# Staged row maxima from 256 keys and 256 key differences instead of 512 keys

## The chip, the cores and the metric

The kernel runs on one core of a Trainium2 chip. The core has a matrix engine (TensorE, PE in the profile, with its weight loads as PEld), a vector engine (VectorE, DVE), a scalar engine (ScalarE, ACT), a general engine (GpSimd, POOL) and a queue that issues transfers (SyncE, SP). ACT can issue transfers as well, from the same in-order queue as its arithmetic. All engines share an on-chip memory (SBUF) of 128 partitions; PE writes its results to PSUM, which DVE and ACT can read. The metric is the device time of one execution in microseconds.

## The reference, cut to what matters

A transformer block: layer norm, attention with 32 heads of 20 columns over 2048 tokens of width 640, a residual, a second layer norm and a SwiGLU feed-forward part.

```
qkv    = layernorm(x) @ wqkv
scores = einsum("bhqd,bhkd->bhqk", q, k) * 20 ** -0.5
p      = softmax(scores, axis=-1)
o      = einsum("bhqk,bhkd->bhqd", p, v)
h      = x + o @ wo
h2     = h + (silu(layernorm(h) @ w_gate) * (layernorm(h) @ w_up)) @ w_down
```

The softmax needs, for every query and head, the maximum over all 2048 keys. All of it is float32; the kernel forms float32 products on PE from a high and a low part of each operand.

## The kernel before, in words

Tokens are cut into four chunks of 512 (`NC`, `CH`) and heads into eight groups of four (`NG`, `G`). One group with one chunk of queries is a *unit* (32 units). The kernel has three stages: the projections (to about 338 us), the attention with the output projection beside it, and the feed-forward part.

**The projections** run over the four chunks. Each chunk has 18 slots: ten *blocks* (`query_key`, L413), each giving 128 output rows of keys (even `m`) or queries (odd `m`) for 512 tokens in 15 matmuls, and eight *value* slots (`value`, 15 matmuls of 320 columns, L469). The first chunk alternates keys and queries; later ones do the five key blocks first and the five query blocks next (the last chunk puts the values between). In the second half of each of the first three chunks, `flip` (L386, transposes at L389) turns the next chunk's normalised tokens.

A block ends in `keep` (L444): ACT and DVE (before slot 8) or ACT and GpSimd (from slot 8) split the result into a high and a low part in one of three buffers `e`, and it is stored to the DRAM tensor `qk_d` of its chunk. `split` is at L79 to L81, `split_sbuf` (a copy out of PSUM first, L265) at L263. The store is issued from ACT's queue (L410), one slot late: `store` issues what the call before has left.

Attention needs the maxima before its exponentials. A part of them is computed inside the projections, 208 *pairs*: one pair is two score matmuls of 128 queries by 512 keys (two heads, 60 rows each, L171, in the two halves of a `ps_wide` tile; three such tiles rotate) and one DVE reduction over both halves (`max_pair`, L175). 60 pairs take keys and queries from the resident tiles `k_stk` and `q_stk` (`unit_keys`); the other 148 take them from *staged* tiles `raw`, 512 keys or 512 queries of one group, read back from `qk_d` (`load_items`, `stack`, issued by SP). Four staged tiles rotate; the next is loaded when all pairs of the fourth before are out. The staged pairs cover groups 1 to 7 for the first chunk's queries and keys, and for the second chunk's queries the keys of the first and a part of the second chunk.

The order is written by hand (`tc.manual_schedule()`): each engine runs its instructions in program order. `visit(n)` puts up to n ready pairs at a place in that order: three after every block or value slot, and, from the second chunk on, one inside each block (after the ninth matmul). In a slot the order is: matmuls, `keep` or the evacuation of the values (L475), `visit(3)`, transfers for the resident tiles, one or two steps of the next chunk's norm on DVE, a flip. So ACT's queue holds a block's copy, split and store issues ahead of anything that the pairs of `visit(3)` bring.

Of the kernel before, what the change touches and what calls it, by code (L numbers as in the profile page):

```python
# [9 lines left out]
F32 = mybir.dt.float32  # L10
# [7 lines left out]
P = 128  # L18
# [11 lines left out]
G = 4  # L30
# [4 lines left out]
ROW = P // 2  # L35
HALF = D // 2
EPS = 1e-5
GD = G * DH

ORDER = ("SmsSMMsWMm", "SsSmWmMs", "SssMWmS")  # L40
# [3 lines left out]
def tile_block(ctx: ExitStack, tc: tile.TileContext, x, wqkv, wo, wg, wu, wd, out):  # L44
# [3 lines left out]
    ctx.enter_context(tc.manual_schedule())  # L48

    dram = ctx.enter_context(tc.tile_pool(name="dram", bufs=1, space=bass.MemoryType.DRAM))  # L50
    qk_d = [dram.tile([2, NG, 2, GD, CH], F32R, name=f"qk_d{c}") for c in range(NC)]
    v_d = dram.tile([S, NG, VG], F32, name="v_d")
    o_d = dram.tile([D, S], F32, name="o_d")
    r_d = dram.tile([H, S], F32, name="r_d")
# [78 lines left out]

    ends = {}

    def stack(dst, which, g, cs):

        src = qk_d[cs.start // CH][which, g].bitcast(F32).rearrange("i (d h) c -> (i d) h c", h=G)
        for b in range(2):
            heads = src[:, 2 * b : 2 * b + 2]  # L140
            both, first = ((DH, 0), (0, 2 * DH))[which]
            for row, n in ((both, 2 * DH), (first, DH)):
                nc.sync.dma_start(
                    dst[b * ROW + row : b * ROW + row + n].bitcast(F32), heads[:n]
                )

    def load_keys(g, cs):

        k = keys[g] = k_stk[g % 2]
        stack(k[:, :, cs], 1, g, cs)  # L150

    def load_queries(u):

        g, c = divmod(u, NC)
        q = queries[u] = stk.tile([P, 2, CH], F32R, name="q_stk", tag="q_stk", bufs=4)
        stack(q, 0, g, slice(c * CH, (c + 1) * CH))

    def load_values(g, t0=0, t1=NT):
        values[g] = v_stk[g % 2]
# [6 lines left out]
    def max_pair(mx, q, k, pair, t, kc, k0):  # L166

        ps = ps_wide()
        for b in range(2):
            rows = slice(b * ROW, b * ROW + NPART)  # L170
            nc.tensor.matmul(  # L171
                ps[:, b, :], q[rows, pair, t * P : (t + 1) * P], k[rows, pair, k0 : k0 + CH],
                start=True, stop=True,
            )
        nc.vector.tensor_reduce(mx[:, :, pair, t, kc], ps, axis=AX.X, op=ALU.max)  # L175

    def max_one(u, kc, t, pair, b):

# [62 lines left out]
    evp_ctx = ExitStack()  # L241
    evp = evp_ctx.enter_context(tc.tile_pool(name="evp", bufs=2))
    evs = [evp.tile([P, NG, VG], F32, name=f"ev{i}", bufs=1) for i in range(2)]
    es = [evp.tile([P, 2, CH], F32R, name=f"e{i}", bufs=1) for i in range(2)]
    es.append(v_stk[0].rearrange("p t w -> p (t w)")[:, : 2 * CH].bitcast(F32R))
    third = es[2] = es[2].rearrange("p (i n) -> p i n", i=2)

    def next_e():
# [3 lines left out]
    with tc.tile_pool(name="pa", bufs=2) as pa:  # L252
# [36 lines left out]
        def load_items():  # L289
            for n, (which, g, c, loaded, _) in enumerate(items):  # L290
                if loaded is not None:
                    continue
                if slot[0] < stored_at(which, g, c) or (n >= 4 and users[n - 4]):
                    return
                t = raw_tile().rearrange("p a b -> p (a b)")[:, : 2 * CH].rearrange(
                    "p (h n) -> p h n", h=2
                )
                stack(t, which, g, slice(c * CH, (c + 1) * CH))
                items[n][3:] = t, slot[0]

        def staged_keys(g, c, kc):
            k, q = place[1, g, (c, kc)], place[0, g, c]

            def one(t, pair):
                max_pair(mxs[g * NC + c], items[q][3], items[k][3], pair, t, kc, 0)
                for n in (k, q):
                    users[n] -= 1
                load_items()

            def ready():  # L310
                return all(items[n][3] is not None and slot[0] >= items[n][4] + 2 for n in (k, q))

            pairs = [(t, pair) for t in moved(g * NC + c, kc) for pair in range(2)]
            for n in (k, q):
                users[n] += len(pairs)
            return [(ready, lambda a=a: one(*a)) for a in pairs]
# [69 lines left out]
        def flip(c, k):  # L386
            ps = ps_one()
            for t in range(TPC):
                nc.tensor.transpose(  # L389
                    ps[:, t * P : (t + 1) * P], xs[c * TPC + t][:, k * P : (k + 1) * P], ident  # L390
                )
            z_hi, z_lo = (z[:, k, :] for z in zs[c])
            split_sbuf(ps, z_hi, z_lo, next_e()[:, 0].bitcast(F32))

        def flip_tokens(t):

# [47 lines left out]
        def keep(c, m, ps):  # L444

            e = next_e()
            if slot[0] < 8:
                split(ps, e[:, 0], e[:, 1], nc.vector)
            else:
                split_sbuf(ps, e[:, 0], e[:, 1], e[:, 1].bitcast(F32))  # L450
            r0 = m // 2 * P
            pieces, r = [], r0
            while r < r0 + P:
                g, i = divmod(r, GD)
                n = min(GD - i, r0 + P - r)
                dst = qk_d[c][1 - m % 2, g].bitcast(F32).rearrange("i r c -> r i c")
                pieces.append((dst[i : i + n], e[r - r0 : r - r0 + n].bitcast(F32)))
                r += n
            store(*pieces, queue=nc.sync if (c, m) == (NC - 1, 2 * ND - 1) else nc.scalar)

        def value(c, t, half):
# [1153 lines left out]
```

## Time and profile before

| | |
|---|---|
| median of the runs shown | 2105.66 us (2105.11 to 2111.35, three runs) |
| the profiled execution's own time | 2112.59 us |
| its span | 2110.5 us |
| granted PE clock, mean | 0.998 |
| projections | from the start to about 338 us |
| DVE reductions of the 208 pairs (L175) | 240.3 us in all |
| ACT in 150 to 200 us | 14.13 of 50 us |

How to read the rows: in a timeline row stand the start, the duration, the engine, the line, what it writes and reads, and how many instructions are merged (x). A bracket gives the idle time before it and what ended that. In a row by groups, the numbers behind the bar are the total busy time and the mean duration in ns, then the idle time before the group and its releasers. The duration of a matmul is modelled and overlaps the next one, so PE's pace is read from start to start.

### The profile page before, as it was taken

How to read it: one execution, taken by the hardware profiler on the slowest of the kernel's cores; microseconds unless marked ns; L12 is line 12 of the kernel's file. 1: busy time of each engine (PE TensorE's matmuls, PEld its weight loads, DVE VectorE, ACT ScalarE, POOL GpSimd, SP SyncE). 2: the span in 40 equal slices, each digit the busy share in tenths (PEclk: the TensorE clock that was granted, in tenths of full speed). 3: DMA queues.
4: the chain of work that ended last, by engine and by line, in shares of the span. 5: the costliest groups of instructions: out<-in, count | busy, mean ns of one | idle time of the engine just before them, and what ended most of it. 6: DMA issues, size and time to landing. Idle time of an engine off the chain costs nothing.

```text
span 2110.5 us, 35624 instructions
## 1 busy us (share of the span) xinstructions
PE 2077.2 (98%) x12636; PEld 1206.5 (57%) x12636; DVE 1753.9 (83%) x2907; ACT 1295.8 (61%) x2571; POOL 694.3 (33%) x1003
## 2 busy tenths in 40 slices
PE   7999999999999999999999999999999999999998
PEld 6666675333333333333333333335578888888888
DVE  7999897999999999999999999996458766666677
ACT  3222216999999998999999999996743222212221
POOL 1122212243343433353420001001135534663555
PEclk9999999999999999999999999999999999999999
DMA  8565532433442524534432113132137755884542
GB/s 260 162 183 167 155 122 82 122 121 107 141 124 97 176 84 133 168 134 131 134 112 70 38 35 90 34 92 84 35 121 258 266 170 187 298 303 158 194 153 94
DMA packets 191633, 295.27 MB, mean 140 GB/s; under 512 B 46840, under 2 KB 81656, under 8 KB 190432
## 3 DMA queue, kind: packets, MB, share of 16 engines
q1 hardware_dynamic: 177872, 266.77, 39.3%
q10 hardware_dynamic: 13584, 26.23, 4.0%
q8 instruction: 101, 1.65, 0.3%
q14 instruction: 76, 0.62, 0.1%
HBM read 196.44 MB, written 95.68 MB: 138 GB/s over the span
## 4 chain that ended last, share of the span: by engine, by line
PE 88%; DVE 6%; DMA 3%; SPq 1%; issue 0%; ACT 0%; POOL 0%; ACTq 0%; POOLq 0%; DVEq 0%
PE acc L917 24%; PE ps_a L1080 15%; PE ps_max L181 15%; PE ps_one L907 15%; PE ps_b L1174 8%; PE ps_one L419 4%; DVE mx L175 4%; PE ps_one L469 2%; PE ps_wide L171 2%; PE ps_max L645 2%; DMA qk_d<-e 1%; PE ps_b L645 1%; DVE mx L187 1%; PE ps_one L389 0%; DMA halves<-j_d 0%
## 5 line engine op out<-in xcount | busy, mean ns | idle before, releaser
L913 ACT ACTIVATE probs<-ps_one 128x512 f32<-128x512 f32 x2048 | 1045.4, 623 | 131.8 <-PE ps_one L907 127.4
L187 DVE TENSOR_REDUCE mx<-ps_max 128x1 f32<-128x512 f32 x1632 | 1020.1, 682 | 96.3 <-PE ps_max L181 54.3
L907 PE MATMUL ps_one<-q_stk,k_stk 62*128 62x512 f32 x2048 | 550.8, 421 | 0.7 <-ACT e L265 0.7
L917 PE MATMUL acc<-probs,v_stk 128*32 128x512 f32 x4096 | 545.2, 605 | 0.3
L181 PE MATMUL ps_max<-k_stk,q_stk 60*128 60x512 f32 x1632 | 540.9, 459 | 2.4 <-DVE mx L187 1.5
L181 PEld LDWEIGHTS ps_max<-k_stk,q_stk 60*128 60x128 f32 x1632 | 230.4, 184 | 428.1 <-DVE mx L187 412.4
L907 PEld LDWEIGHTS ps_one<-q_stk,k_stk 62*128 62x128 f32 x2048 | 299.8, 185 | 81.2 <-ACT probs L913 52.1
L175 DVE TENSOR_REDUCE mx<-ps_wide 128x2 f32<-128x1024 f32 x208 | 240.3, 1216 | 17.6 <-PE ps_wide L171 17.3
L1295 DVE TENSOR_TENSOR tmp<-ps_a,tmp 128x512 f32<-128x512 f32 x208 | 141.2, 689 | 120.1 <-PE ps_a L1080 93.2
L1174 PE MATMUL ps_b<-halves,yp 128*128 128x320 f32 x1032 | 179.3, 308 | 1.9 <-DMA halves<-j_d 1.2
L1174 PEld LDWEIGHTS ps_b<-halves,yp 128*128 128x128 f32 x1032 | 165.1, 188 | 18.5 <-POOL yp L81 1.5
L917 PEld LDWEIGHTS acc<-probs,v_stk 128*32 128x32 f32 x4096 | 80.6, 108 | 160.3 <-issue 152.2
L1080 PE MATMUL ps_a<-t,units 128*128 128x512 f32 x624 | 162.5, 396 | 0.0
L198 POOL CAST both<-neg 128x16 fp32r<-128x16 f32 x32 | 6.6, 206 | 465.0 <-DVE neg L194 222.7
L1080 PE MATMUL ps_a<-z,units 128*128 128x512 f32 x516 | 133.8, 394 | 0.0
L1080 PEld LDWEIGHTS ps_a<-t,units 128*128 128x128 f32 x624 | 112.6, 188 | 18.6
L81 POOL TENSOR_TENSOR yp<-y,yp 128x256 fp32r<-128x256 f32 x96 | 60.2, 627 | 188.1 <-ACT yp L80 188.1
L1179 DVE TENSOR_TENSOR h<-ps_b,h 128x320 f32<-128x320 f32 x248 | 109.9, 480 | 6.8 <-PE ps_b L1174 5.4
L1080 PEld LDWEIGHTS ps_a<-z,units 128*128 128x128 f32 x516 | 93.1, 187 | 15.9
L1080 PE MATMUL ps_a<-z,lasts 128*128 128x512 f32 x324 | 92.5, 393 | 0.0
L80 ACT ACTIVATE yp<-tmp 128x512 fp32r<-128x512 f32 x40 | 25.3, 632 | 103.1 <-POOL tmp L1167 103.1
L265 ACT ACTIVATE e<-ps_one 128x512 f32<-128x512 f32 x31 | 18.5, 598 | 110.0 <-PE ps_one L419 83.0
(169 smaller groups left out, 2059.8 us busy)
## 6 DMA issues: line engine op xcount, KB each, us to landing
units<-w_d SPq DMA_DIRECT2D x186, 256.0 KB
w_d<-stage SPq DMA_DIRECT2D x106, 256.0 KB
halves<-j_d SPq DMA_DIRECT2D x70, 320.0 KB
j_d<-stage SPq DMA_DIRECT2D x42, 320.0 KB
raw<-qk_d SPq DMA_DIRECT2D x70, 160.0 KB
k_stk<-qk_d SPq DMA_DIRECT2D x64, 160.0 KB
q_stk<-qk_d SPq DMA_DIRECT2D x64, 160.0 KB
rb<-r_d SPq DMA_DIRECT2D x32, 256.0 KB
```

The costliest lines, as they stand in the source:

```text
L175: nc.vector.tensor_reduce(mx[:, :, pair, t, kc], ps, axis=AX.X, op=ALU.max)
L181: nc.tensor.matmul(ps, queries[u][rows, pair, t * P : (t + 1) * P], keys[u // NC][rows, pair, kc * CH : (kc + 1) * CH], start=True, stop=True,
L187: nc.vector.tensor_reduce(mxs[u][:, b, pair, t, kc : kc + 1], ps, axis=AX.X, op=ALU.max)
L419: nc.tensor.matmul(ps, w[:, k, m * P : (m + 1) * P], a[:, k, :], start=(n == 0 and k == 0), stop=(n == 2 and k == ND - 1),)
L645: nc.tensor.matmul(ps[:, :HALF], a[:, k, :], w[:, k, hs], start=(n == 0), stop=(n == 3 * ND - 1),)
L907: nc.tensor.matmul(ps, keys[u // NC][rows, p, kt * P : (kt + 1) * P], queries[u][rows, p, :], start=True, stop=True,)
L913: nc.scalar.activation(probs[p][:, b, :], ps, AF.Exp, scale=scale)
L917: nc.tensor.matmul(acc[32 * j : 32 * j + 32, :], values[u // NC][:, kt, j * VW : j * VW + 32], probs[j // 2][:, j % 2, :], start=(kt == 0) ...
L1080: nc.tensor.matmul(ps.rearrange("p (t n) -> p t n", t=TPC), w[k][:, i], z[k][:, :, j], start=(first and m == 0), stop=(last and m == len(n ...
L1174: nc.tensor.matmul(ps, a, b, start=(n == 0), stop=(n == len(pairs) - 1))
L1179: nc.vector.tensor_tensor(out=h, in0=ps, in1=h, op=ALU.add)
L1295: add = lambda out, ps, x: nc.vector.tensor_tensor(out=out, in0=ps, in1=x, op=ALU.add)
```

## The change

Keys of the first two chunks are stored with 256 further columns: for columns i of 0 to 255, key i less key i + 256. `qk_d` becomes two tensors, `q_d` and `k_d`; `k_d` has 768 columns in the first two chunks. A staged key tile now holds columns 256 to 767, that is the second 256 keys and the 256 differences; a score matmul keeps its shape. For a query, the score of a difference is the difference of the two scores, and max(a, b) = b + max(a - b, 0). So in the staged pairs ACT takes the positive part of the 2 x 256 difference scores into an SBUF tile `over` (two rotate), and DVE, once per head, adds it to the 256 scores in PSUM and takes the maximum in the same instruction. The 60 pairs from the resident tiles are as before.

In `keep`, key blocks before slot 8 get a second copy out of PSUM (ACT), a subtraction from PSUM (DVE), and a split by ACT and GpSimd. Key blocks from slot 8 on, in the first two chunks, get a subtraction on GpSimd between the copy and the split, and the split covers 768 columns. Query blocks and the keys of the last two chunks are stored as before. The buffers `e` grow by half, and the parameter `dynamic_dma_scratch_size` is set to 8192, which frees on-chip memory.

```
+LOWEST = -3.4028234e38
...
-    qk_d = [dram.tile([2, NG, 2, GD, CH], F32R, name=f"qk_d{c}") for c in range(NC)]
+    q_d = [dram.tile([NG, 2, GD, CH], F32R, name=f"q_d{c}") for c in range(NC)]
+    k_d = [
+        dram.tile([NG, 2, GD, CH + (CH // 2 if c < 2 else 0)], F32R, name=f"k_d{c}")
+        for c in range(NC)
+    ]
...
-    def stack(dst, which, g, cs):
+    def stack(dst, which, g, c, cols=slice(0, CH)):
 
-        src = qk_d[cs.start // CH][which, g].bitcast(F32).rearrange("i (d h) c -> (i d) h c", h=G)
+        src = (q_d, k_d)[which][c][g].bitcast(F32).rearrange("i (d h) c -> (i d) h c", h=G)
         for b in range(2):
-            heads = src[:, 2 * b : 2 * b + 2]
+            heads = src[:, 2 * b : 2 * b + 2, cols]
...
+    def max_halves(mx, q, k, pair, t, kc):
+
+
+        ps = ps_wide()
+        for b in range(2):
+            rows = slice(b * ROW, b * ROW + NPART)
+            nc.tensor.matmul(
+                ps[:, b, :], q[rows, pair, t * P : (t + 1) * P], k[rows, pair, :],
+                start=True, stop=True,
+            )
+        over = evp.tile([P, 2, CH // 2], F32, name="over")
+        nc.scalar.activation(over, ps[:, :, CH // 2 :], AF.Relu)
+        for b in range(2):
+            nc.vector.tensor_tensor_reduce(
+                over[:, b], ps[:, b, : CH // 2], over[:, b], 1.0, LOWEST, ALU.add, ALU.max,
+                mx[:, b, pair, t, kc : kc + 1],
+            )
...
-    es = [evp.tile([P, 2, CH], F32R, name=f"e{i}", bufs=1) for i in range(2)]
-    es.append(v_stk[0].rearrange("p t w -> p (t w)")[:, : 2 * CH].bitcast(F32R))
+    EW = CH + CH // 2
+    es = [evp.tile([P, 2, EW], F32R, name=f"e{i}", bufs=1) for i in range(2)]
+    es.append(v_stk[0].rearrange("p t w -> p (t w)")[:, : 2 * EW].bitcast(F32R))
...
-                stack(t, which, g, slice(c * CH, (c + 1) * CH))
+                stack(t, which, g, c, slice(CH // 2, EW) if which else slice(0, CH))
...
-                max_pair(mxs[g * NC + c], items[q][3], items[k][3], pair, t, kc, 0)
+                max_halves(mxs[g * NC + c], items[q][3], items[k][3], pair, t, kc)
...
         def keep(c, m, ps):
 
             e = next_e()
+            which, half, n = 1 - m % 2, CH // 2, CH
+            hi, lo = e[:, 0], e[:, 1]
+            copy = lo.bitcast(F32)
+            over = copy[:, CH:]
             if slot[0] < 8:
-                split(ps, e[:, 0], e[:, 1], nc.vector)
+                split(ps, hi[:, :CH], lo[:, :CH], nc.vector)
+                if which:
+                    nc.scalar.activation(over, ps[:, half:], AF.Copy)
+                    nc.vector.tensor_tensor(
+                        out=over, in0=ps[:, :half], in1=over, op=ALU.subtract
+                    )
+                    split(over, hi[:, CH:], lo[:, CH:], nc.gpsimd)
             else:
-                split_sbuf(ps, e[:, 0], e[:, 1], e[:, 1].bitcast(F32))
+                nc.scalar.activation(copy[:, :CH], ps, AF.Copy)
+                if which and c < 2:
+                    nc.gpsimd.tensor_tensor(
+                        out=over, in0=copy[:, :half], in1=copy[:, half:CH], op=ALU.subtract
+                    )
+                    n = EW
+                split(copy[:, :n], hi[:, :n], lo[:, :n], nc.gpsimd)
+            n = EW if which and c < 2 else CH
...
-                dst = qk_d[c][1 - m % 2, g].bitcast(F32).rearrange("i r c -> r i c")
-                pieces.append((dst[i : i + n], e[r - r0 : r - r0 + n].bitcast(F32)))
-                r += n
+                dst = (q_d, k_d)[which][c][g].bitcast(F32).rearrange("i r c -> r i c")
+                pieces.append((dst[i : i + w], e[r - r0 : r - r0 + w, :, :n].bitcast(F32)))
+                r += w
...
-    nc = _bacc.Bacc("TRN2", target_bir_lowering=False, num_devices=1)
+    nc = _bacc.Bacc(
+        "TRN2", target_bir_lowering=False, num_devices=1, dynamic_dma_scratch_size=8192
+    )
```

More of the change, by code (lines that the diff above doesn't have):

```diff
@@ L149, in load_keys @@
         k = keys[g] = k_stk[g % 2]
-        stack(k[:, :, cs], 1, g, cs)
+        stack(k[:, :, cs], 1, g, cs.start // CH)
     def load_queries(u):
@@ L155, in load_queries @@
         q = queries[u] = stk.tile([P, 2, CH], F32R, name="q_stk", tag="q_stk", bufs=4)
-        stack(q, 0, g, slice(c * CH, (c + 1) * CH))
+        stack(q, 0, g, c)
     def load_values(g, t0=0, t1=NT):
@@ L392, in flip @@
             z_hi, z_lo = (z[:, k, :] for z in zs[c])
-            split_sbuf(ps, z_hi, z_lo, next_e()[:, 0].bitcast(F32))
+            split_sbuf(ps, z_hi, z_lo, next_e()[:, 0, :CH].bitcast(F32))
         def flip_tokens(t):
@@ L454, in keep @@
                 g, i = divmod(r, GD)
-                n = min(GD - i, r0 + P - r)
-                dst = qk_d[c][1 - m % 2, g].bitcast(F32).rearrange("i r c -> r i c")
-                pieces.append((dst[i : i + n], e[r - r0 : r - r0 + n].bitcast(F32)))
-                r += n
+                w = min(GD - i, r0 + P - r)
+                dst = (q_d, k_d)[which][c][g].bitcast(F32).rearrange("i r c -> r i c")
+                pieces.append((dst[i : i + w], e[r - r0 : r - r0 + w, :, :n].bitcast(F32)))
+                r += w
             store(*pieces, queue=nc.sync if (c, m) == (NC - 1, 2 * ND - 1) else nc.scalar)
```

## The prediction

> **What bounds the kernel now.** I read the page first, then the stretches of the span, the groups of instructions of the projections, PE's timeline slot by slot, and the chain of waits. From the page:
>
> ```profile
> PE 2077.2 (98%) x12636; PEld 1206.5 (57%) x12636; DVE 1753.9 (83%) x2907; ACT 1295.8 (61%) x2571; POOL 694.3 (33%) x1003
> ```
>
> PE is the limit over the whole, but the change touches only the projections, which end near 338 us. One stretch of them (columns: PE, PEld, DVE, ACT and POOL busy, then clock, DMA share, GB/s):
>
> ```profile
> 150.00:200.00 50.00, 49.00 (x271) 35.67 (x268) 47.61 (x48) 14.13 (x25) 11.61 (x9) 1.00 0.50 163
> ```
>
> DVE is busy for 48 of 50 us, PE for 49, ACT for 14. A faster DVE is worth only what PE waits for it, and that is read from PE's own order. A clean stretch of query or key blocks:
>
> ```profile
> 274.35 0.96 PE L171 MATMUL ps_wide<-raw 60*128 60x512 f32 x6
> ...
> 277.54 0.50 PE L171 MATMUL ps_wide<-raw 60*128 60x512 f32 x2
> ...
> 279.56 0.97 PE L171 MATMUL ps_wide<-raw 60*128 60x512 f32 x6
> ```
>
> The first and the last row are bursts of three pairs of score matmuls after a block, the middle one the single pair inside the next block ("mid"), 3.19 us after the burst began. One block takes 279.56 - 274.35 = 5.21 us and PE never waits in it: an infinitely fast DVE would not shrink it. A clean value slot, with the flip (L389) of one column block in it:
>
> ```profile
> 75.44 0.97 PE L469 MATMUL ps_one<-w_hi,z_hi 128*128 128x320 f32 x5
> ...
> 78.70 0.65 PE L389 MATMUL ps_one<-ident,xt 128*128 128x128 f32 x4
> 79.11 0.97 PE L469 MATMUL ps_one<-w_hi,z_hi 128*128 128x320 f32 x5
> ```
>
> That is 3.67 us, of which the flip holds 0.41, so 3.26 without one.
>
> **What the removed waits are worth.** These places are not clean:
>
> ```profile
> 57.95 1.00 PE L469 MATMUL ps_one<-w_hi,z_hi 128*128 128x320 f32 x5
> ...
> 71.76 0.97 PE L469 MATMUL ps_one<-w_hi,z_hi 128*128 128x320 f32 x5
> ...
> 186.95 1.43 PE L419 MATMUL ps_one<-z_hi,w_hi 128*128 128x512 f32 x5
> 209.22 1.43 PE L419 MATMUL ps_one<-z_hi,w_hi 128*128 128x512 f32 x5
> ...
> 242.19 0.49 PE L171 MATMUL ps_wide<-raw 60*128 60x512 f32 x2 [0.63 <-DVE mx L175]
> ```
>
> 57.95 to 71.76 holds three value slots, the last with a flip: 13.81 us, clean 3.26 + 3.26 + 3.67 = 10.19. That is **-3.6 us** to gain. At 242.19 PE's third pair comes 1.1 after it would in a clean burst (three pairs in 0.9): **-1.1**. From 186.95 to 209.22 four blocks take 5.57 each instead of 5.21. The other waits on DVE in this stage stand mostly before pairs that read the resident keys, which the change leaves as they are. So the prize is small: 5 us, 8 with the blocks.
>
> **The change part by part.** The rows that price the parts, and after them the chain of waits at the start:
>
> ```profile
> L175 DVE TENSOR_REDUCE mx<-ps_wide 128x2 f32<-128x1024 f32 x208 | 240.3, 1216 | 17.6 <-PE ps_wide L171 17.3
> L171 PE MATMUL ps_wide<-raw 60*128 60x512 f32 x296 | 59.2, 458 | 8.9 <-DVE mx L175 4.4 <-DMA raw<-qk_d 3.7 <-DMA qk_d<-e 0.4
> L1179 DVE TENSOR_TENSOR h<-ps_b,h 128x320 f32<-128x320 f32 x248 | 109.9, 480 | 6.8 <-PE ps_b L1174 5.4
> L81 DVE TENSOR_TENSOR kept<-ps_a,kept 128x128 fp32r<-128x128 f32 x8 | 2.3, 283 | 1.0 <-ACT kept L80 0.9
> L90 DVE TENSOR_TENSOR t_a<-r_a 128x4 f32<-128x4 f32 x12 | 1.9, 162 | 0.4
> L475 ACT ACTIVATE ev<-ps_one 128x320 f32<-128x320 f32 x32 | 14.0, 438 | 63.9 <-PE ps_one L469 54.9 <-DMA qk_d<-e 5.0 <-DMA qk_d<-z_hi 3.2
> L757 POOL TENSOR_TENSOR sums<-raw 128x256 f32<-128x256 f32 x13 | 9.5, 732 | 111.8 <-DMA raw<-in_B_w_up 111.8
> ```
>
> ```profile
> 23.25 0.70 DVE e L81
> 23.97 7.18 DMA qk_d<-e
> 31.98 4.94 DMA k_stk<-qk_d
> 36.94 4.66 DMA q_stk<-qk_d
> 41.61 4.99 DMA qk_d<-e
> 46.71 0.61 ACT e L80
> 47.34 0.69 DVE e L81
> 48.03 3.39 DVE mx L175 x3
> 25.00:30.00 5.00, 5.00 (x23) 4.13 (x22) 4.01 (x8) 3.33 (x5) 0.00 (x0) 1.00 1.01 333
> ```
>
> *The staged maximum on DVE.* 148 of the 208 pairs change (296 matmuls of staged tiles). Three reductions on the chain take 3.39, so 1.13 each, 0.08 less than one's busy time: neighbours overlap by that. An add of 128x256 from PSUM and SBUF lies between the rows of 128x128 and 128x320: 0.283 + 0.197 x 128/192 = 0.41. Two of them cost 0.67 at the best, with the overlap; at the worst 0.83 and two small instructions of 0.16 to bring the maximum out, 1.15. No row shows this operation; I take 0.75, near the lower end, because it reads its operands as the add does and its neighbours are of its own kind. DVE then saves 148 x 0.38 = 56 us of work, most of which PE never waited for.
>
> [...]
>
> *The positive part on ACT.* A 128x512 read of PSUM takes 0.61 (46.71), so 148 x 0.61 = 90 us more; there is room. But the queue is in order, and the positive parts of a burst stand behind the evacuation, the split and the store issues of the block just ended:
>
> ```profile
> 192.00 2.25 ACTq L410 DMA_DIRECT2D qk_d<-e  x3
> 275.15 0.82 ACTq L410 DMA_DIRECT2D qk_d<-e  x2
> ...
> 280.36 1.36 ACTq L410 DMA_DIRECT2D qk_d<-z_hi  x3
> ```
>
> Counted from the burst's start (274.35, 279.56), the issues end after 1.6 with two stores and after 2.15 with three; held as at 192.00, after 3. I take 2.0. The first buffer is then free at 2.0 + 0.6 + 0.1 + 0.75 + 0.1 = 3.55 (0.1 for each handover). There are three PSUM buffers, so the mid pair, due at 3.19, needs this one: **0.4 us of PE wait per block**, where today the reduction starts at once. Ends: nothing with two quick stores, 1.4 behind a held queue. There are 14 such places: nine with a norm step on DVE, where part of the wait is already in the 5.57 and I count 0.3, five at 0.42: **+4.8**.
>
> *Key blocks of the second chunk* (five, from 90 us). ACT must also wait for a GpSimd difference of 128x256 (0.73, and two handovers) and make a split half as long again (0.2): the first positive part comes 1.0 later, the wait is 1.4 per block, 7.0 in all. But one load is late there today:
>
> ```profile
> 113.24 0.76 PE L171 MATMUL ps_wide<-raw 60*128 60x512 f32 x1 [1.05 <-DMA raw<-qk_d]
> ```
>
> A PE that comes later waits less for it. Bounds 2 and 7; I take **+4.2**.
>
> *The first blocks.* For the first chunk's keys before slot 8 a second PSUM copy, a subtraction, a second split and a GpSimd subtraction go ahead of the store, which grows by half. The first store now leaves at 23.97, after DVE's 23.95. Behind that come the subtraction 0.41, the split about 0.4 (0.61 for twice the columns, less than halved) and GpSimd 0.73, with handovers 25.65: +1.7. Each of three key stores that lie on the chain or share its stream brings 0.26 MB more, 0.8 to 0.9 at the 333 GB/s then reached: +2.8. **+4.5** in all reach the first maxima at 48.03, behind which PE waits. Ends: 0, if other queued transfers fill the gaps, and 8, if every store is half as long again. The additional ACT and DVE work there (0.8 and 0.4, four times) lies inside the waits for these stores.
>
> *Counted at nothing.* GpSimd's longer second halves (768 columns for 512) end before the next block's store call 5 us later; without that cover each would hold ACT's queue by 0.7. Staged loads read as many bytes as before, out of wider rows. Two tensors for one, the wider ring and the smaller scratch issue no instruction. In a slot with a flip ACT now does an evacuation, three positive parts, a copy and a split, 0.44 + 3 x 0.61 + 0.6 + 0.6 = 3.5 of 3.67: full, but not over. Attention and feed-forward start earlier or later and are otherwise the same.
>
> **Sum**, against the profiled execution's own 2112.6: -3.6 - 1.1 + 4.8 + 4.2 + 4.5 = +8.8, or 2121.4. That execution lies 6.9 above the median of the runs shown, 2105.66; on the median's footing the sum gives 2114.5, +0.42%.
>
> **Rivals.** First, *faster*: ACT's queue is free in time. If the first positive part starts by 1.6 after the burst, as behind the two stores at 275.15, the mid pair never waits; the nine blocks become clean (-3.2), the key blocks and first blocks hide in the waits for DMA, and the sum is -3.6 - 1.1 - 3.2 = -7.9: 2098. For it: ACT is idle for 36 of 50 us. Against it: the rows with three stores, and the one held for 2.25. It is decided at a release by 3.19. Chance 0.19. Second, *no difference*: gains and losses cancel, for instance with the first blocks at 0 and the key blocks at 2 (+2.1): 2100 to 2112. For it: no term is above 5 us. Chance 0.26. Third, *DVE is not relieved*: at 1.15 a pair the gains of 4.7 go, and the 19 places lose 0.4 more each: 8.8 + 4.7 + 7.6 = +21, 2127. For it: no row shows this operation cheap. Against it: the add rows. Chance 0.13. My own case (2112 to 2121) keeps 0.42.
>
> **How the numbers follow.** About 0.3%, 6.3 us, is what a measurement of this kernel can tell from no change. Slower: 0.42 + 0.13 = 0.55; within 0.26; faster 0.19. The range goes from 2097, a little past the faster rival, to 2131, the third rival with a held queue; about one in ten lies beyond each end.
>
> **What would show it.** Two DVE operations of 128x256 per staged pair, at 0.33 to 0.41 each (near 0.58 the third rival holds). PE's mid pairs waiting for DVE by about 0.4, and by 1 to 1.5 between 95 and 118 us. Value slots after 60 us at 3.3. DVE's first maxima about 4 us after 48.03. The last projection matmul near 347 instead of 338. If blocks keep 5.2 and the projections end before 335, my reading of ACT's order is wrong; if the first store leaves within 0.5 us of 23.97, the first blocks are; if DVE's pair takes 1.1, the price is.

## The result, and the profile after

The changed kernel takes 2118.54 us in the median (2116.87 to 2121.55, seven runs) against 2108.7 us (2105.11 to 2114.98, seven runs) of the kernel before, measured beside it: a ratio of 1.0043, with a 95% interval from 1.0029 to 1.0058. The forecast was +0.42%. The profiled execution took 2118.48 us with a span of 2116.7 us, 6.2 more than the span before.

The view by groups of instructions, for the changed kernel's first 360 us on VectorE (total busy time and mean ns of one behind the first bar, idle time ahead behind the second), and the row of the positive part from its page:

```profile
L195 DVE CUSTOM_DVE_ANT_0 over<-ps_wide,over 128x256 f32<-128x256 f32 x296 | 109.7, 420 | 82.1 <-ACT over L193 79.6
L180 DVE TENSOR_REDUCE mx<-ps_wide 128x2 f32<-128x1024 f32 x60 | 69.4, 1218 | 2.0 <-PE ps_wide L176 1.7
L195 DVE DVE_READ_ACCUMULATOR2_ANT mx<- 128x1 f32 x296 | 24.6, 83 | 0.0
...
L193 ACT ACTIVATE over<-ps_wide 128x512 f32<-128x512 f32 x148 | 84.0, 597 | 46.1 <-DVE mx L195 18.6
```

The change does what it says: 148 pairs went from one reduction to two adds with a maximum, and VectorE's busy time over the whole kernel fell from 1753.9 to 1695.8 us. Yet VectorE is now idle for 79.6 us because the positive part (`over`) isn't there yet: the pair no longer needs PE and VectorE alone, but ScalarE in between. That idle time isn't the price itself. The price is what PE waits for in turn, and the next rows show it.

Next the timeline of PE in the first chunk: the blocks that wait, the first resident maxima, and the first and the fourth value slot. First the kernel before, then the changed one:

```profile
23.99 1.43 PE L419 MATMUL ps_one<-z_hi,w_hi 128*128 128x512 f32 x5 [0.82 <-DVE e L81]
...
41.68 1.43 PE L419 MATMUL ps_one<-z_hi,w_hi 128*128 128x512 f32 x5 [0.37 <-DVE v_stk L81]
...
45.30 0.96 PE L171 MATMUL ps_wide<-k_stk,q_stk 60*128 60x512 f32 x6
```

```profile
23.88 1.45 PE L443 MATMUL ps_one<-z_hi,w_hi 128*128 128x512 f32 x5 [1.70 <-DVE e L479]
...
31.71 1.42 PE L443 MATMUL ps_one<-z_hi,w_hi 128*128 128x512 f32 x5 [0.69 <-DVE v_stk L479]
...
40.42 1.43 PE L443 MATMUL ps_one<-z_hi,w_hi 128*128 128x512 f32 x5 [1.62 <-DVE e L479]
...
44.51 1.43 PE L443 MATMUL ps_one<-z_hi,w_hi 128*128 128x512 f32 x5 [0.37 <-DVE v_stk L86]
...
48.14 0.97 PE L176 MATMUL ps_wide<-k_stk,q_stk 60*128 60x512 f32 x6
...
61.36 1.00 PE L510 MATMUL ps_one<-w_hi,z_hi 128*128 128x320 f32 x5
...
72.26 0.97 PE L510 MATMUL ps_one<-w_hi,z_hi 128*128 128x320 f32 x5
```

Line 479 is the new subtraction, which reads PSUM. A block's PSUM buffer is free only when it is done, and there are two such buffers, so PE waits three times for it; before, it waited 0.82 at the first of these places and not at all at the other two. The three value slots from 61.36 take 10.90 us; before, those from 57.95 took 13.81. That is the gain of the change, 2.9 us.

The mid pairs (two matmuls inside a block) behind the second chunk's key blocks:

```profile
98.33 0.50 PE L188 MATMUL ps_wide<-raw 60*128 60x512 f32 x2 [0.61 <-DVE mx L195]
...
104.66 0.50 PE L188 MATMUL ps_wide<-raw 60*128 60x512 f32 x2 [1.08 <-DVE mx L195]
...
112.07 0.50 PE L188 MATMUL ps_wide<-raw 60*128 60x512 f32 x2 [1.42 <-DVE mx L195]
...
118.58 0.50 PE L188 MATMUL ps_wide<-raw 60*128 60x512 f32 x2 [0.36 <-DVE mx L195]
...
125.24 0.49 PE L188 MATMUL ps_wide<-raw 60*128 60x512 f32 x2 [0.69 <-DVE mx L195]
```

And one block of the last chunk across the engines, a burst of three pairs at 284.65 and the mid pair of the block after it:

```profile
284.65 0.96 PE L188 MATMUL ps_wide<-raw 60*128 60x512 f32 x6
284.75 0.60 ACT L484 ACTIVATE e<-ps_one 128x512 f32<-128x512 f32 x1 [0.88 <-PE ps_one L443]
285.38 0.63 ACT L85 ACTIVATE e<-e 128x512 fp32r<-128x512 f32 x1
285.45 1.37 ACTq L434 DMA_DIRECT2D k_d<-z_hi  x3
...
286.92 1.09 ACT L193 ACTIVATE over<-ps_wide 128x512 f32<-128x512 f32 x2 [0.90 <-issue]
287.55 0.43 DVE L195 CUSTOM_DVE_ANT_0 over<-ps_wide,over 128x256 f32<-128x256 f32 x1 [2.86 <-ACT over L193]
...
288.47 0.49 PE L188 MATMUL ps_wide<-raw 60*128 60x512 f32 x2 [0.59 <-DVE mx L195]
```

ScalarE copies the block, splits it, issues three stores, and only 2.27 us after the burst begins makes the first positive part. VectorE stands idle for 2.86 us, the first PSUM buffer comes free late, and the mid pair waits 0.59. Worst is one place in the third chunk, where three stores hold the queue for 2.32 us:

```profile
197.71 2.32 ACTq L434 DMA_DIRECT2D k_d<-e  x3
200.13 1.08 ACT L193 ACTIVATE over<-ps_wide 128x512 f32<-128x512 f32 x2 [2.87 <-PE ps_one L443]
...
201.64 0.59 PE L188 MATMUL ps_wide<-raw 60*128 60x512 f32 x2 [1.83 <-ACT over L193]
```

The burst there begins at 195.89, the first positive part comes 4.2 us later, and the mid pair waits 1.83. Where the times went, from start to start in the two timelines:

| stretch | before | after | change |
|---|---|---|---|
| to the first value slot | 57.95 | 61.36 | +3.4 |
| three value slots | 13.81 | 10.90 | -2.9 |
| second chunk, key blocks (89.84 to 120.35 before) | 30.51 | 31.99 | +1.5 |
| second chunk, query blocks (to 146.92) | 26.57 | 28.13 | +1.6 |
| second chunk, values (to 176.59) | 29.67 | 30.65 | +1.0 |
| third chunk, blocks (to 234.78) | 58.19 | 58.85 | +0.7 |
| last chunk, key blocks (264.87 to 290.90) | 26.03 | 27.34 | +1.3 |
| last chunk, values (to 318.92) | 28.02 | 29.37 | +1.4 |
| start of the attention | 338.67 | 346.26 | +7.6 |

The stretches left out change by 0.1 us at most. Each of the two executions has two stretches of 3.4 us in which PE's granted clock is 0.50: before at 113.2 and 215.6 us, after at 55.6 and 202.4. By an estimate from these figures each is worth up to 1.7 us, so a single row of the table can be off by that, while the two totals hold the same.

### The profile page after: what moved, and what is told of

Same layout as the page of the kernel before. It is cut to its first block, busy times and chain, and to the rows that moved or that the text cites. A ratio compares the mean times of both kernels' runs of the same rounds, so it can differ in the third digit from the quotient of the medians.

```text
span 2116.7 us, 36528 instructions
## 1 busy us (share of the span) xinstructions
PE 2077.2 (98%) x12636; PEld 1207.4 (57%) x12636; DVE 1695.8 (80%) x3355; ACT 1381.2 (65%) x2727; POOL 707.1 (33%) x1013
## 4 chain that ended last, share of the span: by engine, by line
PE 89%; DVE 4%; DMA 2%; ACT 2%; POOL 1%; issue 1%; ACTq 1%; SPq 0%; POOLq 0%; DVEq 0%
PE acc L958 24%; PE ps_one L948 15%; PE ps_a L1121 15%; PE ps_max L204 15%; PE ps_b L1215 8%; PE ps_one L443 4%; PE ps_one L510 3%; PE ps_max L686 2%; PE ps_wide L188 1%; PE ps_b L686 1%; DVE mx L180 1%; DVE over L195 1%; DVE mx L210 1%; PE ps_wide L176 1%; ACT over L193 1%
## 5 line engine op out<-in xcount | busy, mean ns | idle before, releaser
L195 DVE CUSTOM_DVE_ANT_0 over<-ps_wide,over 128x256 f32<-128x256 f32 x296 | 109.7, 420 | 82.1 <-ACT over L193 79.6
L193 ACT ACTIVATE over<-ps_wide 128x512 f32<-128x512 f32 x148 | 84.0, 597 | 46.1 <-DVE mx L195 18.6
```

The costliest lines, as they stand in the source:

```text
L193: nc.scalar.activation(over, ps[:, :, CH // 2 :], AF.Relu)
L195: nc.vector.tensor_tensor_reduce(over[:, b], ps[:, b, : CH // 2], over[:, b], 1.0, LOWEST, ALU.add, ALU.max, mx[:, b, pair, t, kc : kc + 1],)
```

## The experiments

Times in this section are medians; the kernel before ran beside each, at 2110.4 to 2111.2 us. The changed kernel did not run again beside them. Where a run is set against it, its 2118.5 us is from the first measurement, in which the kernel before took 2108.7; so such a distance is uncertain by some 2.5 us. By so much at most it changes when it is formed from the two ratios to the kernel before.

**The two halves of the change, each alone.** First only the storing of differences:

```
-                max_halves(mxs[g * NC + c], items[q][3], items[k][3], pair, t, kc)
+                max_pair(mxs[g * NC + c], items[q][3], items[k][3], pair, t, kc, 0)
...
-                stack(t, which, g, c, slice(CH // 2, EW) if which else slice(0, CH))
+                stack(t, which, g, c, slice(0, CH))
```

> Differences of keys are computed and stored as in the changed kernel, but the staged pairs load the 512 plain columns and use one reduction on VectorE as before. My theory: the first chunk starts its maxima 3 to 3.5 us late, the value slots keep their 13.8 us, the blocks keep their 5.2 to 5.6; 3 to 5 us slower than the kernel before. Rival, the producers are hidden by the late loads of the second chunk: within 1 us of the kernel before.

Then only their use, on plain columns:

```
-                if which:
+                if False:
...
-                if which and c < 2:
+                if False:
...
-            n = EW if which and c < 2 else CH
+            n = CH
```

> Keys are stored as before, without differences, and the staged pairs use the positive part, the add and the maximum on the plain columns, so that those maxima are not the real ones. My theory: value slots between 57 and 72 us take 10.9 instead of 13.8 us (-2.9), blocks still lose 3 to 5 us to ScalarE's order: between -1 and +2 us against the kernel before. Rival, the consumer carries the whole loss and the differences cost nothing: +4 to +8. Second rival, the consumer is a pure gain and the differences carry the loss: -3 to -5.

Storing alone took 2118.23 us, a ratio of 1.0036 (1.0022 to 1.0051): 7.6 us, more than the 3 to 5 expected. Use alone took 2111.37, 1.0005 (0.9992 to 1.0017), as expected: its gain in the value slots (10.8 us for 13.8) and its losses behind them (4.7 us in sum from the second chunk's query blocks on) nearly cancel. The two add up to 0.41%, against 0.43% for both. The runs of storing alone had a mean granted clock of 0.9967, and those of the kernel before 0.9977; a straight line through the times and clocks of these runs and all runs of the kernel before gives 1.9 us for 0.001 of clock. So some 2 us of the 7.6 go with the clock. The rest, 5.7, lies just above what I expected, and in the profile the attention starts 4.3 us later than before.

**The first chunk's early differences left out.**

```
-                if which:
+                if False:
                     nc.scalar.activation(over, ps[:, half:], AF.Copy)
...
-            n = EW if which and c < 2 else CH
+            n = EW if which and c < 2 and slot[0] >= 8 else CH
```

> As the changed kernel, but the four key blocks of the first chunk that are stored early are stored plain (the later ones keep their differences), and the staged pairs read the plain 512 columns, so that their maxima are not the real ones. My theory (the early differences delay the first store and its stream): first resident maxima near 45 instead of 48 us, and 3 to 4 us faster than the changed kernel, near 2115. Rival, what is won there is lost to loads later: within 1 us of the changed kernel.

2114.39 us, 1.0013 (1.0004 to 1.0022), so 4.1 below the changed kernel (6.3 by the ratios), as my theory had it. The timeline of PE of this run:

```profile
23.99 1.43 PE L443 MATMUL ps_one<-z_hi,w_hi 128*128 128x512 f32 x5 [0.82 <-DVE e L86]
...
30.92 1.29 PE L443 MATMUL ps_one<-z_hi,w_hi 128*128 128x512 f32 x5
...
41.46 1.43 PE L443 MATMUL ps_one<-z_hi,w_hi 128*128 128x512 f32 x5 [0.17 <-DVE v_stk L86]
...
45.08 0.97 PE L176 MATMUL ps_wide<-k_stk,q_stk 60*128 60x512 f32 x6
```

The waits of 1.70, 0.69, 1.62 and 0.37 are down to 0.82 and 0.17, which is 3.4 less, and the first maxima come at 45.08 instead of 48.14. In these two traces the delay thus shows in full as PE's waits for its PSUM buffers. Its size varies from run to run: in the profiles of seven kernels that make the early differences in this way, the changed one among them, the first resident maxima come between 48.14 and 50.15 us, and in five that make none between 44.90 and 45.42. The means are 4.1 us apart.

**The same differences made without touching PSUM.**

```
-                    nc.scalar.activation(over, ps[:, half:], AF.Copy)
-                    nc.vector.tensor_tensor(
-                        out=over, in0=ps[:, :half], in1=over, op=ALU.subtract
-                    )
-                    split(over, hi[:, CH:], lo[:, CH:], nc.gpsimd)
+                    d = evp.tile([P, 2, half], F32, name="over")
+                    h, w = hi.bitcast(F32), lo.bitcast(F32)
+                    gp(out=d[:, 0], in0=h[:, :half], in1=h[:, half:CH], **sub)
+                    gp(out=d[:, 1], in0=w[:, :half], in1=w[:, half:CH], **sub)
+                    gp(out=d[:, 1], in0=d[:, 0], in1=d[:, 1], op=ALU.add)
+                    nc.gpsimd.tensor_copy(d[:, 0].bitcast(F32R), d[:, 1])
+                    gp(out=d[:, 1].bitcast(F32R), in0=d[:, 1], in1=d[:, 0], **sub)
...
+                if which and slot[0] < 8:
+                    more.append((dst[i : i + w, :, CH:], d[r - r0 : r - r0 + w]))
```

> The changed kernel with the early differences of the first chunk made apart: the four key blocks before slot 8 are split and stored plain, as in the kernel before; GpSimd then makes the differences from the two halves of the split in five instructions into a buffer of their own, and they are stored one block later. My theory (the second PSUM copy and subtraction hold the two PSUM buffers of the projections and the store): PE's waits of 1.70, 0.69 and 1.62 us in the first blocks shrink, the first maxima come 2 to 3 us earlier, and of the 4.1 us that leaving these differences out brought, 2 to 3 are won: near 2116. Rival, the bytes carry the delay: within 1 us of the changed kernel.

2120.63 us, 1.0042 (1.0029 to 1.0056): nothing was won in all. The timelines of ScalarE and PE say why:

```profile
39.91 1.70 ACTq L434 DMA_DIRECT2D k_d<-over  x3
41.66 0.74 ACT L85 ACTIVATE w_hi<-raw 128x640 fp32r<-128x640 f32 x1 [4.63 <-DMA k_d<-over]
...
43.91 1.42 PE L443 MATMUL ps_one<-z_hi,w_hi 128*128 128x512 f32 x5 [2.15 <-DVE v_stk L86]
...
56.70 4.71 ACTq L434 DMA_DIRECT2D k_d<-over  x3
61.53 0.60 ACT L488 ACTIVATE e<-ps_one 128x512 f32<-128x512 f32 x1 [5.80 <-DMA k_d<-over]
```

The wait for the subtraction is gone, and the stores that came apart hold ScalarE's queue: it idles 4.63 us ahead of a weight's split, the next block's split comes late, and PE waits 2.15 us for its PSUM buffer. The first maxima come at 47.55, 0.6 earlier than in the changed kernel's profile and 1.7 earlier than the mean of the seven, so the freed buffers bring something. It is lost again in the value slots: three more stores of differences hold the queue for 4.71 us, ScalarE idles 5.80 ahead of 61.53, and the three slots take 13.58 us instead of 10.90. My theory left out the queue of ScalarE. Whether the bytes make these issues so long isn't shown.

**The positive parts ahead of the block's copy, split and stores** (chunks two to four).

```
-            keep(c, m, ps)
+            if c == 0:
+                keep(c, m, ps)
+            return ps
...
                 visit(3)
+                if c and kind == "block":
+                    keep(c, *which, ps)
```

> The changed kernel with one thing moved: in chunks two to four a block's evacuation, split and stores are issued after the staged pairs that follow the block, not before them. My theory (the positive parts stand behind that work in ScalarE's queue): the first positive part of a burst starts right behind its matmuls, the mid pairs' waits of 0.4 to 1.4 us go, blocks of the last chunk return from 5.75 to 5.2 us, and the kernel is 4 to 7 us faster than the changed one (2118.5), near 2113. Rival, VectorE's chain or the two buffers of the positive part set the waits: within 1.5 us of the changed kernel. A third way, the evacuation comes too late for its PSUM buffer or for the stores: slower than the changed kernel.

2117.99 us, 1.0036 (1.0023 to 1.005): within 1 us of the changed kernel, so the rival's figure. The last chunk's timeline shows that the mechanism wasn't the rival's:

```profile
281.50 0.97 PE L188 MATMUL ps_wide<-raw 60*128 60x512 f32 x6
282.04 1.09 ACT L193 ACTIVATE over<-ps_wide 128x512 f32<-128x512 f32 x2 [1.35 <-PE ps_wide L188]
...
284.75 1.51 ACTq L434 DMA_DIRECT2D k_d<-e  x2
...
286.36 0.60 ACT L193 ACTIVATE over<-ps_wide 128x512 f32<-128x512 f32 x1 [1.04 <-issue]
...
287.91 0.49 PE L188 MATMUL ps_wide<-raw 60*128 60x512 f32 x2 [0.46 <-ACT over L193]
```

The first positive part of the burst is in time (282.04), and the mid pair doesn't wait. But now copy, split and stores stand ahead of the mid pair's positive part, which comes at 286.36, and the last pair of the next burst waits 0.46. Here the wait has moved by three pairs. Over the whole, from 90 us to the attention, PE's waits for VectorE in the staged pairs fall from 8.4 to 4.2 us, but one late load, at 202.25, now holds PE for 3.46, where the changed kernel's profile has no wait for a load.

**The block's copy out of PSUM on VectorE**, in the changed kernel, and then in the kernel that only uses differences.

```
-                nc.scalar.activation(copy[:, :CH], ps, AF.Copy)
+                nc.vector.tensor_copy(copy[:, :CH], ps)
```

> The changed kernel with one instruction moved: after the first chunk's early blocks a block is copied out of PSUM by VectorE, not by ScalarE. The run that moved this work behind the staged pairs only moved the wait: the store issues then held the next positive part. So my theory is now ScalarE's fullness and not its order: a block gives it a copy of 0.59, a split of 0.63, two or three issues of 0.5 and four positive parts of 0.6, 4.6 to 5.1 of 5.2 us. With 0.6 taken off, mid pairs wait at most 0.1, blocks of the last chunk take 5.2 to 5.3, and the kernel is 2 to 4 us faster than the changed one, near 2115. Rival, VectorE's chain: the copy of 0.6 stands ahead of the adds, and the kernel is as fast as the changed one or slower.

> No differences of keys (the staged maxima are taken on plain columns and are not the real ones), positive part, add and maximum as in the changed kernel, and the PSUM copy of the blocks on VectorE. Without that move the same kernel ran as fast as the kernel before (2111.4 against 2110.7). If ScalarE's fullness takes there what the value slots win, this one is 2 to 4 us faster than the kernel before. Rival, VectorE's chain sets the blocks: no gain against it.

2129.6 us, 1.0084 (1.0071 to 1.0098), and 2122.44 us, 1.0047 (1.0035 to 1.006): both 11 us slower by the medians, and 9 by the ratios, than the same kernel without the move. That was the rival's sign, and my theory that ScalarE's fullness alone counts fell. The last chunk in the first of the two:

```profile
294.87 0.97 PE L188 MATMUL ps_wide<-raw 60*128 60x512 f32 x6
294.97 0.69 DVE L484 COPY e<-ps_one 128x512 f32<-128x512 f32 x1
...
295.70 0.63 ACT L85 ACTIVATE e<-e 128x512 fp32r<-128x512 f32 x1 [1.60 <-DVE e L484]
295.76 1.37 ACTq L434 DMA_DIRECT2D k_d<-z_hi  x3
...
297.24 1.09 ACT L193 ACTIVATE over<-ps_wide 128x512 f32<-128x512 f32 x2 [0.90 <-ACT e L85]
...
298.79 0.50 PE L188 MATMUL ps_wide<-raw 60*128 60x512 f32 x2 [0.66 <-DVE mx L195]
```

ScalarE is less busy, and its first positive part is later than before the move: 2.37 us after the burst, for 2.27. The split must wait for VectorE, and everything behind the split with it. So the move brings nothing here, but the last chunk's key blocks hold only 0.4 of that in the profiles (27.7 us for 27.3). Most of the loss, 6.5, lies in the second chunk's query blocks (30.4 for 28.1) and the third chunk's blocks (63.1 for 58.9), where VectorE also makes the next chunk's norm steps. From 90 us to the attention PE's waits for VectorE in the staged pairs rise from 8.4 to 14.0. So VectorE's own load counts as well, and the runs don't separate it from the wait of ScalarE's queue.

**The rounded copy of the split on GpSimd**, from which nothing comes back to ScalarE within the block.

```
-                split(copy[:, :n], hi[:, :n], lo[:, :n], nc.gpsimd)
+                nc.gpsimd.tensor_copy(hi[:, :n], copy[:, :n])
+                nc.gpsimd.tensor_tensor(
+                    out=lo[:, :n], in0=copy[:, :n], in1=hi[:, :n].bitcast(F32), op=ALU.subtract
+                )
```

> The changed kernel with one instruction moved: after the first chunk's early blocks the first half of the split (the rounded copy, 0.63 of ScalarE's time per block) is made by GpSimd, which makes the second half already. Unlike the copy on VectorE, nothing then goes back to ScalarE within the block. My theory (the first positive part of a burst comes too late behind copy, split and issues): it now starts 0.6 earlier, the mid pairs' waits behind three stores shrink from 0.6 to about 0, and the kernel is 2 to 4 us faster than the changed one, near 2115. Rival, GpSimd's longer queue (2.6 per block, 4.4 behind the second chunk's key blocks) delays the stores and so ScalarE's queue: no gain, or slower.

2111.99 us, 1.0 (0.9991 to 1.0009): 6.5 us below the changed kernel (9.1 by the ratios), more than the 2 to 4 expected, and level with the kernel before. The last chunk:

```profile
279.32 0.97 PE L188 MATMUL ps_wide<-raw 60*128 60x512 f32 x6
279.43 0.60 ACT L484 ACTIVATE e<-ps_one 128x512 f32<-128x512 f32 x1 [0.94 <-PE ps_one L443]
279.49 1.30 ACTq L434 DMA_DIRECT2D k_d<-z_hi  x3
...
280.09 0.61 POOL L490 CAST e<-e 128x512 fp32r<-128x512 f32 x1 [3.23 <-ACT e L484]
...
280.79 1.29 POOL L491 TENSOR_TENSOR e<-e 128x512 fp32r<-128x512 f32 x1
280.91 1.09 ACT L193 ACTIVATE over<-ps_wide 128x512 f32<-128x512 f32 x2 [0.89 <-POOL e L490]
...
282.52 0.50 PE L188 MATMUL ps_wide<-raw 60*128 60x512 f32 x2
```

Behind three stores the first positive part now starts 1.59 us after the burst, and the mid pair has no wait. All five key blocks of the last chunk take 5.22 us, where two of the changed kernel's took 5.85 and 5.74. PE's waits for VectorE in the staged pairs, from 90 us to the attention, fall from 8.4 to 2.4 us. From the first value slot to the attention this profile takes 275.2 us, the changed kernel's 284.9 and the one before 280.7: here the change gains 5.5 us on the kernel before, up to 1.7 of it by one slow stretch fewer, and the late first value slot (63.99 for 57.95) takes that back.

The same move in the kernel before, as a control:

> The kernel before with the rounded copy of the split on GpSimd, and nothing else of the change. My theory: ScalarE is not late for anything there, so nothing changes, within 1.5 us of the kernel before. Rival, the shorter queue of ScalarE helps any kernel of this kind: 2 us or more faster, and then the staged maxima in halves still lose by that much.

2116.01 us, 1.0024 (1.0012 to 1.0035): slower, as neither theory had it. So the gain above is not one that any kernel gets from the move. What costs 5 us here isn't settled. In its profile the attention starts at 340.0, 1.3 later than before, and three slow stretches of PE's clock lie ahead of it and a longer one behind, where the kernel before has two:

```profile
62.60:66.00 3.40, 3.40 (x13) 0.50 0.11 40
113.80:117.20 3.40, 3.40 (x9) 0.50 0.54 185
216.20:219.60 3.40, 3.40 (x10) 0.50 0.54 166
342.50:349.30 6.80, 6.80 (x27) 0.50 0.51 149
```

(Columns of this view by windows: the stretch, its length, PE's busy time, the granted clock, the share of the DMA engines, GB/s.) At half the clock, by an estimate from these rows, they are worth up to 8.5 us together, against 3.4 in the profile before. By the mean clock of all runs, 0.9966 against 0.9980, it is some 2.7 us. So the clock may be most of this loss, but what lowers it isn't shown.

**Fewer differences.** The second chunk's keys plain:

```
-                max_halves(mxs[g * NC + c], items[q][3], items[k][3], pair, t, kc)
+                if kc:
+                    max_pair(mxs[g * NC + c], items[q][3], items[k][3], pair, t, kc, 0)
+                else:
+                    max_halves(mxs[g * NC + c], items[q][3], items[k][3], pair, t, kc)
...
-                if which and c < 2:
+                if which and c < 1:
```

> Differences for the keys of the first chunk alone; the second chunk's keys are stored plain and their pairs use the one reduction as before. All maxima are the real ones. My theory: the waits of 0.6 to 1.4 us behind the second chunk's key blocks shrink to 0.4 and those of the later chunks go, the first chunk's delay of 3.4 us stays: 2 to 4 us faster than the changed kernel, near 2115, still slower than the kernel before. Rival, the second chunk's differences cost nothing (their waits stand in place of a late load): within 1 us of the changed kernel.

2116.94 us, 1.0026 (1.0018 to 1.0035): 1.6 below the changed kernel, between the two theories and too close to decide. The key blocks of the second chunk are shorter, as expected (89.96 to 118.39, 28.4 us instead of 32.0), but the last chunk loses as in the changed kernel: 26.6 us for its key blocks and 29.8 for its values, for 27.3 and 29.4 there.

With GpSimd's rounded copy besides:

> The rounded copy on GpSimd, as in the run that came out equal to the kernel before, and differences for the keys of the first chunk alone; the second chunk's keys are stored plain and their pairs use the one reduction. All maxima are the real ones. By my theory what is left of the loss is the first chunk's 4 us, balanced by the value slots; without the second chunk's differences its key blocks return to 5.2 us: 0 to 2 us faster than the kernel before. Rival, nothing is lost there any more: equal to it.

2111.6 us, 1.0002 (0.9993 to 1.0011): equal to the kernel before. And the version put together to beat both, with GpSimd's rounded copy, differences for the first chunk's keys alone and the early ones made apart:

```
-                max_halves(mxs[g * NC + c], items[q][3], items[k][3], pair, t, kc)
+                if c:
+                    max_pair(mxs[g * NC + c], items[q][3], items[k][3], pair, t, kc, 0)
+                else:
+                    max_halves(mxs[g * NC + c], items[q][3], items[k][3], pair, t, kc)
```

> A version put together from what the runs showed: differences are made for the keys of the first chunk alone, apart on GpSimd as in the run beside this one; the positive part, add and maximum are used only for the pairs of first-chunk queries with first-chunk keys, which hold the value slots between 57 and 86 us, and all others use the one reduction; the rounded copy of the split is made by GpSimd. All maxima are the real ones. By my theory the value slots keep their gain of 3 to 4.5 us, the first chunk costs about 1, and the later chunks run as before: 1 to 4 us faster than the kernel before. If the gain of the value slots is taken back by the loads of the second chunk: equal to the kernel before within 1 us.

2113.36 us, 1.0015 (1.0006 to 1.0024): not faster. Its first value slot starts at 62.04, 4.1 later than before and no earlier than in the seven kernels named above (61.11 to 63.99), and that takes back the 2.4 us that the three slots win. No version that ran beats the kernel before.

## Why the prediction was right

The sign and the size held (+0.43% for a forecast of +0.42%), and the sum's largest parts are where it put them, though no term is exact. That the ratio meets the forecast to 0.01% is luck: the interval alone spans 0.29 to 0.58%, and terms that were too high made up for losses that the sum left out.

- *The staged maximum on DVE*, 0.75 a pair: the adds follow each other at 0.345 us (two begin at 283.92 and 284.26 in the changed kernel's timeline), so a pair takes 0.69, near the lower end of 0.67. The saving of VectorE is 58 us, for 56. The third rival is out. The small instructions that its worst end, 1.15, added are there, 296 accumulator reads of 83 ns, one for each add, where my estimate had two of 0.16 a pair. But each begins 0.07 to 0.08 us before its add ends, in 194 cases at the same time as the next add (both at 283.92, say), and costs no step of its own here.
- *The value slots*, -3.6: measured -2.9. The slots take 3.3, 3.9 and 3.7; I had 3.3, 3.3 and 3.7. In the second a pair still waits 0.34 us for VectorE.
- *The wait at 242.19*, -1.1: not won. The stretch of the third chunk's values gains 0.1, and a pair there now waits 0.53 us for a positive part.
- *The positive part behind copy, split and stores*, +4.8: the blocks concerned lost 1.6, 0.7 and 1.3, so 3.5 in the sum of the unrounded times. The place, the order of the queue, the three-store case (the mid pair at 288.47 is late by 0.59) and the held queue (1.83 at 201.64, for 1.4) are as forecast. The spread is not: of the mid pairs behind these blocks only three wait more than 0.1 us, the third at 294.22 with 0.50, where I had 0.3 to 0.4 at each of 14 places. The third pairs of four bursts wait some 0.4 besides. That the sums are near is partly luck. The condition, a release by 3.19 with a first positive part by 1.6, is confirmed from the other side by the run with GpSimd's copy: at 1.59 there is no wait. In the changed kernel's last chunk there is none behind starts of up to 1.72 either, and waits of 0.50 and 0.59 behind 2.17 and 2.27. What I had not seen is that another order doesn't help: copy, split and issues are one lump, 0.60, 0.63 and up to 1.4 us, and in the last chunk moving it only picked another pair that stands behind it. With four positive parts of up to 0.6 such a block gives ScalarE up to 5.0 of 5.2 us, but that this fullness is the cause isn't shown: with 0.6 of it moved to VectorE the kernel was slower.
- *Key blocks of the second chunk*, +4.2: measured +1.5. The mid waits behind these blocks are 0.61, 1.08, 1.42, 0.36 and 0.69, so 4.2 in sum and at most the 1.4 that I priced for each. But the late load at 113.24 vanished altogether, and the profile before has a slow stretch of the clock at 113.2 us that the changed kernel's doesn't have there. As that is worth up to 1.7, what the change costs here lies between 1.5 and 3.2, and the bound of 2 isn't refuted.
- *The first blocks*, +4.5: 3.4 in the trace, 4.1 by the median of the run without them, and 4.1 between the means of the profiles. The size is right and the mechanism only half: I priced a later and larger store (the first leaves at 25.20 instead of 23.97, so 1.2 later for 1.7), and PE waits for PSUM buffers that the subtraction holds. The run that freed them lost in the value slots what it won, since more store issues hold ScalarE's queue. How much the bytes alone cost stays open.
- *Counted at nothing*: two places were not. The value slots of the second and of the last chunk lost 1.0 and 1.4, most of it in the first slot behind the blocks (4.2 us for 3.3, and 4.7 for 3.6).

In the projections the terms thus sum to 7.6 at the attention's start, for 8.8. The span is longer by only 6.2, the ratio corresponds to 9.1 us and the medians differ by 9.8. What gives back 1.4 us behind the attention's start in the profile stays open.

## What to carry to other kernels

When a step is handed to a second engine, write down that engine's whole queue for one period of the loop, issues of transfers included, and see what stands ahead of the new step; a mean load of 28% said nothing here, while the start of the first positive part did: at 1.59 us behind the burst PE didn't wait, at 2.27 it did. In these runs the worth of a relief also depended on who took the work: 0.6 us a block off ScalarE lost 9 to 11 us on VectorE, for which ScalarE's split then waited (1.60 at 295.70), and won 6.5 to 9 on GpSimd; how much of the loss is VectorE's own load isn't separated. And here a producer that held a PSUM buffer for one more read was paid for by PE (waits of 1.70, 0.69 and 1.62 us), not by the engine that reads.

## What the hardware showed besides

In the changed kernel two activations of 128x512 from PSUM, each 0.60 us by its row, take 1.09 together where they follow each other (at 286.92), so the second ends 0.49 after the first. In the run with the rounded copy on GpSimd, that engine rounds 128x512 from SBUF in 0.61 us (at 280.09) but takes 1.29 for a subtraction of the same size (at 280.79).

In the profiles of this case PE's granted clock falls to 0.50 for stretches of 3.4 or 6.8 us, which a window of 10 us shows as 0.83 (110 to 120 us in the profile before) or 0.66. Apart from the last few us of the span, all of them lie between 41 and 360 us, at other times in each kernel; at half the clock they are worth, by estimate, from 0 to 8.5 us in the fourteen profiled executions. The runs' mean clock differs with the kernel: 0.9988 over the 12 runs that only use differences, 0.9966 over the 12 of the control, the kernel before with GpSimd's copy. The one profiled execution with no such stretch, that of the kernel that only uses differences, had no gap of PE above 1.1 us from 24 us to the attention, but a gap of 2.9 us at 194 us in the control was followed by one only at 216 us, and the one at 62.6 us there had no gap above 0.8 us near it. So what triggers them isn't shown. For single profiles it means that several us between two kernels can be the clock alone, and that only many runs decide effects of this size.
